# Repacking two transposed weights from six groups on 112 partitions to five groups on 128

## The chip, the cores and the metric

One core of one Trainium2 chip. The metric is the time of one execution on the device, in microseconds (us). Executions that the host times are some 2.1 us longer than the span that the profile shows (393.76 against 391.6 for the profiled run of before). In the clock records of the traces, TensorE's clock is granted either in full or in half; what sets it is called the clock gate here, and each run lists the share granted over the whole run. That share matters: runs with 0.996 to 1.0 are called undisturbed, and only those are compared where it is said so.

## The reference, cut to what matters

```python
def reference(A_x, A_wqkv, A_w_phi, A_wo, B_x, B_w1, B_w2, c, w_mod):
    # sa, ca, ga, sb, cb, gb = six rows of silu(c) @ w_mod
    h = _layernorm(x) * (1 + ca) + sa
    x = x + ga * attention(h)      # 32 heads of 18; pq = q @ w_phi[h], pk = k @ w_phi[h], softmax features
    h = _layernorm(x) * (1 + cb) + sb
    x = x + gb * ffn(h)            # relu, 576 -> 4608 -> 576
```

2048 tokens, 576 features, bf16. Since pq = (h @ wq) @ w_phi, the kernel folds w_phi into wq and wk once, head by head, ahead of the projections. ga is about 0.001 in size, so the attention branch hardly shows in the output.

## The kernel before: the parts concerned

The fold multiplies each group of transposed weight rows (as the stationary operand, 116 of its columns at a time, five such chunks) by a block-diagonal matrix of the heads' w_phi. Groups are cut so that none straddles head 16, where the output changes its PSUM bank.

```python
G6 = ((0, 6), (6, 6), (12, 4), (16, 6), (22, 6), (28, 4))     # first head, heads
GR = 108; GP = 112; R = 116; NC = 5; F = NC * R               # F = 580
wkT = carve(R1, 5800, (6, F))          # R1: one region, used by turns
wqT = carve(R1, 9280, (6, F))
...
load(sp, ccol[:], "cc"); load(sp, flat(wsc), "wsc")
load(sp, flat(wkT[0:GP]), "wkT")       # 112 rows of 6960 B
load_xT(0); load(sp, flat(wsh), "wsh"); load_x(0, 2) ...
...
def fold_all(wT):                      # keys: job FK, 30 matmuls
    for ck in range(NC):
        for g, (h0, nh) in enumerate(G6):
            pe.matmul(o, lhsT=wT[0:nf, g, ck * R:(ck + 1) * R], rhs=bdw[0:nf, g, 0:nf], ...)
def fold_mm(wT, ck, pr): ...           # queries: jobs FQ0..FQ4, one chunk each, 6 matmuls

w1a = carve(R1, 0, (4, DFF))           # DFF = 4608; quarter i is columns 4608*i to 4608*(i+1) of R1
def t_part(i, k):                      # VectorE: T1 = B12 - B11 and so on, 6 of 18 groups each
    eng.tensor_tensor(out=o[:, j, :], in0=p[:, j, :], in1=q[:, j, :], op=ALU.subtract)
# "wo" jobs, GpSimd: wo_sb[:, c, :] *= ga_row, five of them
```

The order of all jobs up to the feed-forward part is one written list. Of it, three stretches matter (Z: filler matmuls, which multiply zeros and whose results are not used, sc: modulation, FK: key fold, wl1: load of the second quarter of w1, tp: VectorE's subtractions, nO: attention output):

```python
Z11 sx sd rp sc FK ca Z2 fs0 fsr frr fra2 sh ...
... FQ2:0 pM5 K8:2 ... sp10 wl1 V7:0 ... FQ0:0 pA9 FQ4:2 ...
... tp0 wo4 qt1 kz Q4:1 eQ3 wo2 sq2 tp2 Q5:2 eQ4 sq3 tp1 wo3 nu0:3 eQ5 Q6:0 sq4 nO0 wo0 ...
```

The softmax here doesn't subtract the row's maximum and nothing guards it: scores larger than these inputs give would overflow.

Of the kernel before, what the change touches and what calls it, by code (L numbers as in the profile page):

```python
# [7 lines left out]
P = 128  # L8
BF16 = mybir.dt.bfloat16
# [7 lines left out]
S, D, H, DH, DFF = 2048, 576, 32, 18, 4608  # L17
NT = S // P
NC = 5
R = 116  # L20
F = NC * R
X0 = 96
NX = X0 + 4
NJ = DFF // P
HD = 288
NK = NJ // 2
G6 = ((0, 6), (6, 6), (12, 4), (16, 6), (22, 6), (28, 4))
GR = 108
GP = 112
BLK = ((0, 2), (2, 2), (4, 4), (8, 4), (12, 4))  # L30
E36 = 2 * DH
KVC = [((P * c) // E36, (P * c + P - 1) // E36) for c in range(9)]
# [30 lines left out]
def tile_block(ctx, tc, a, out):  # L63
# [7 lines left out]
    def small(shape, dtype, name):  # L71
        return mem.tile(shape, dtype, name=name, tag=name)

    def carve(reg, start, shape):
        n = 1
        for d in shape:
            n *= d
        names = "abcd"[:len(shape)]
        v = reg[:, start:start + n]
        return v.rearrange(f"p ({' '.join(names)}) -> p {' '.join(names)}", **dict(zip(names, shape)))  # L80

    x_sb = small([P, NT, D], BF16, "x_sb")
    R1 = small([P, 4 * DFF + DFF // 2], BF16, "R1")
# [17 lines left out]

    wsc = carve(R1, 0, (NC, F))
    wsh = carve(R1, 2900, (NC, F))
    wkT = carve(R1, 5800, (6, F))
    wqT = carve(R1, 9280, (6, F))
    wv_raw = carve(R1, 12760, (NC, D))
    wfold = carve(R1, 15640, (NC, D))
    wga = carve(R2[0], 0, (NC, D))
# [7 lines left out]
    mk = small([P, 1], FP32, "mk")  # L116
    mask = small([P, KVW], BF16, "mask")
    epsr = small([1, KVW + P], BF16, "epsr")
    RS = small([P, 6 * GR + NC * NX + NC * P], BF16, "RS")
    bdw = carve(RS, 0, (6, GR))  # L120
    m98 = carve(RS, 6 * GR, (NC, NX))
    rep = carve(RS, 6 * GR + NC * NX, (NC, 32))
    kvz = small([P, KVW], BF16, "kvz")
    ga_row = small([P, D], BF16, "ga_row")
    gb_row = small([P, D], BF16, "gb_row")
# [31 lines left out]
    PS = psum.tile([P, 8, 512], FP32, name="PS")  # L157
# [6 lines left out]
    act, dve, pool, sp, pe = nc.scalar, nc.vector, nc.gpsimd, nc.sync, nc.tensor  # L164
# [24 lines left out]
    def load_xT(b):  # L189
        t0, nt = BLK[b]  # L190
        xT, o, _, _ = XOFF[t0]
        i = t0 * NC * P
        sp.dma_start(xT[:, o:o + NC * nt * P], a["xT"][:, i:i + NC * nt * P])

    def load(eng, dst, name):
        eng.dma_start(dst, a[name])

    def flat(v):
        return v.rearrange("p a b -> p (a b)")

    load(act, flat(bdw[0:GP]), "bdw")
    load(act, ident[:], "ident")
    load(sp, ccol[:], "cc")
    load(sp, flat(wsc), "wsc")
    load(sp, flat(wkT[0:GP]), "wkT")
    load_xT(0)
    load(sp, flat(wsh), "wsh")
    load_x(0, 2)
# [2 lines left out]
    load_xT(1)  # L211
    load_x(4, 2)
    load(sp, epsr[:], "epsr")
    load(sp, flat(wqT[0:GP]), "wqT")
    load_xT(2)
    load(sp, flat(wcb), "wcb")
    load(sp, flat(wsb), "wsb")
# [35 lines left out]
                              rhs=siluc[0:R, ck:ck + 1], start=(ck == 0), stop=(ck == NC - 1))  # L253

    def fold_mm(wT, ck, pr):
        for g, (h0, nh) in enumerate(G6):
            k, c0 = divmod(h0 * DH, HD)
            nf = nh * DH
            pe.matmul(pr[0:R, k, c0:c0 + nf], lhsT=wT[0:nf, g, ck * R:(ck + 1) * R], rhs=bdw[0:nf, g, 0:nf],
                      start=True, stop=True)  # L260

    def v2(ap):
        return ap.rearrange("p (b f) -> p b f", b=2)
# [166 lines left out]
    G5, FW = 504, 72  # L430

    def fold_all(wT):

        for ck in range(NC):
            for g, (h0, nh) in enumerate(G6):
                nf, c0 = nh * DH, h0 * DH
                o = PS[0:R, ck, c0:c0 + nf] if g < 5 else PS[0:R, 5, FW * ck:FW * (ck + 1)]
                pe.matmul(o, lhsT=wT[0:nf, g, ck * R:(ck + 1) * R], rhs=bdw[0:nf, g, 0:nf], start=True, stop=True,  # L438
                          skip_group_check=True)

# [24 lines left out]
    A12, A22 = A2[:, :, 0, :], A2[:, :, 1, :]  # L465
    SS = RS[:, 0:6 * HD].bitcast(FP32).rearrange("p (a f) -> p a f", f=HD)
    X, Y, Z = 6, 4, 7
# [128 lines left out]
    def k_minus(t):  # L596
# [4 lines left out]

    ENG = {"d": dve, "a": act, "p": pool}
    fold_chunk = lambda c, pr: fold_mm(wqT, c, pr)
    ROWS = {"K": wfold, "V": wv_raw, "Q": wfold}
    ROWD = {"K": wk, "V": wv, "Q": wq}
# [7 lines left out]
        "sh": lambda: mods([wsh], None, R, 7, idle=6),  # L613
        "shc": lambda: dve.tensor_copy(m98[0:R, :, X0 + 3], PS[0:R, 7, 0:NC]),
        "FK": lambda: fold_all(wkT),
        "fs": lambda c: f_scaled(wk, c), "fsd": lambda c: f_scaled_d(wk, c),
        "frd": lambda c: f_raw(dve, c), "fra": lambda c: f_raw(act, c),
# [208 lines left out]
def _rows():  # L826

    r = list(range(464 + X0)) + [-1] * (NX - X0) + list(range(464 + X0, D))
    return r + [-1] * (F - len(r))

def _layout(inputs):
    import numpy as np
    g = {k: np.ascontiguousarray(np.asarray(v)) for k, v in inputs.items()}
    dt = g["A_x"].dtype
    rows = np.array(_rows())
    on = rows >= 0

    def pad(m, n):
        return np.concatenate([m, np.zeros((n - m.shape[0],) + m.shape[1:], dt)], axis=0)

    def feat(m):

        z = np.zeros((F, m.shape[1]), dt)
        z[on] = m[rows[on]]
        return pad(z.reshape(NC, R, -1).transpose(1, 0, 2), P)

    def cols(m):
        z = np.zeros((m.shape[0], F), dt)
        z[:, on] = m[:, rows[on]]
        return z  # L850

    def flat(m):
        return np.ascontiguousarray(m).reshape(m.shape[0], -1)

    x = g["A_x"].reshape(S, D)
    o = {"xk": flat(x.reshape(NT, P, D).transpose(1, 0, 2))}
    xt = feat(np.ascontiguousarray(x.T))
    o["xT"] = np.concatenate([flat(xt[:, :, t0 * P:(t0 + nt) * P]) for t0, nt in BLK], axis=1)
    o["cc"] = flat(feat(g["c"].reshape(D, 1)))
    wm = g["w_mod"]  # L860
    sec = [wm[:, i * D:(i + 1) * D] for i in range(6)]
    o["wsc"] = flat(feat(cols(sec[1])))
    o["wsh"] = flat(feat(cols(sec[0])))

    def dup(m):
        return np.concatenate([m, m[:, 512:]], axis=1)
    o["wsb"], o["wcb"] = flat(feat(dup(sec[3]))), flat(feat(dup(sec[4])))
    o["wga"], o["wgb"] = flat(feat(sec[2])), flat(feat(sec[5]))
    w = g["A_wqkv"]

    def groups(m):
        z = np.zeros((6, GR, m.shape[1]), dt)
        for i, (h0, nh) in enumerate(G6):
            z[i, :nh * DH] = m[h0 * DH:(h0 + nh) * DH]
        return flat(pad(z.transpose(1, 0, 2), GP))
    o["wqT"] = groups(np.ascontiguousarray(cols(w[:, 0:D].T.copy())))
    o["wkT"] = groups(np.ascontiguousarray(cols(w[:, D:2 * D].T.copy())))
    o["wv"] = flat(feat(w[:, 2 * D:]))
    bd = np.zeros((6, GR, GR), dt)
    for i, (h0, nh) in enumerate(G6):  # L880
        for h in range(nh):
            bd[i, h * DH:(h + 1) * DH, h * DH:(h + 1) * DH] = g["A_w_phi"][h0 + h]
    o["bdw"] = flat(pad(bd.transpose(1, 0, 2), GP))
    idm = np.zeros((P, P + 1), np.float32)
    idm[:, :P] = np.eye(P)
    idm[[X0 + 1, 29, 61, 93, 125], P] = -1.0
    o["ident"] = idm.astype(dt)
    mk = np.zeros((P, KVW), np.float32)
    ep = np.zeros((1, KVW + P), np.float32)
    ep[0, KVW:] = 1.0  # L890
    for c in range(9):
        k, p0 = KVO[c]
        p0 += KVN[0] * k
        for h in range(KVC[c][0], KVC[c][1] + 1):
            b = p0 + (h - KVC[c][0]) * VW
            r = np.arange(P)
            mk[(P * c + r) // E36 == h, b:b + VW] = 1.0
            ep[0, b + DH] = 0.5e-6
    o["mask"], o["epsr"] = mk.astype(dt), ep.astype(dt)
    wo = np.zeros((NC * P, D), dt)  # L900
    wo[:D] = g["A_wo"]
    o["wo"] = flat(wo.reshape(NC, P, D).transpose(1, 0, 2))
    w1 = g["B_w1"]
    o["w1a"] = flat(w1[:512].reshape(4, P, DFF).transpose(1, 0, 2))
    o["w1b"] = np.concatenate([w1[512:, :DFF // 2], w1[512:, DFF // 2:]], axis=0)
    w2 = g["B_w2"].reshape(NJ, P, D).transpose(1, 0, 2)
    o["w2a"], o["w2b"] = flat(w2[:, :18]), flat(w2[:, 18:])
    return {k: np.ascontiguousarray(v) for k, v in o.items()}
# [19 lines left out]
```

## Time and profile before

| | before |
|---|---|
| time, median of 3 runs | 393.49 us (393.40 to 393.77) |
| span of the profiled run | 391.6 us |
| key fold on TensorE | 9.016 to 10.603 us (first to last start), 30 matmuls |
| first use of the fold by VectorE | 10.84 us |
| TensorE reaches the feed-forward part | 94.38 us |
| packets of wkT, of wqT (mean time of one) | 377 ns, 407 ns |
| packets of wsh, 128 rows of 5800 B | 224 ns |

Packet times are those that the trace records for each row of a transfer. The columns of timelines are: start, duration, instruction, idle time before it and its cause. Two lines of TensorE's list of waits matter below. The columns of TensorE's list of waits are: who waited, for what, us in total, times, longest.

```profile
PE PS L529 <- DVE o_sb L399: 0.8, 1, 0.8
...
PE PS L438 <- DMA R<-in_wkT_dram: 0.5, 1, 0.5
```

The first is a wait for attention's output at 80 us. What stands behind it is this stretch of the timelines of VectorE and of GpSimd (start, duration, instruction, idle time before it and its cause):

```profile
74.93 4.07 DVE L474 TENSOR_TENSOR RT<-R 128x1728 f16<-128x1728 bf16 x2
...
79.30 0.76 DVE L399 TENSOR_TENSOR o_sb<-PS,rden 128x576 bf16<-128x576 f32 x1
...
74.76 7.83 POOL L637 TENSOR_TENSOR wo_sb<-wo_sb,ga_row 128x576 bf16<-128x576 bf16 x5 [1.59 <-DMA ga_row<-gatd]
```

Two subtractions take 2.02 and 2.13 us, while the same instruction took 1.13 at 72.95 us. They run beside the scaling of wo on GpSimd, which began 0.17 us before the first of the two.

### The profile page before, as it was taken

The page shows a single profiled execution, that of the slowest core. Times are in us where ns is not written, and L with a number is a line of the kernel's source. Part 1 is how long each engine was busy: PE and PEld are TensorE (multiplying, and loading weights), DVE is VectorE, ACT ScalarE, POOL GpSimd, SP SyncE. Part 2 cuts the span into 40 slices and gives each one's busy share as a digit, 9 for nine tenths or more (in the row PEclk, how much of TensorE's full clock was granted, in tenths as well). Part 3 has the DMA queues.
Part 4 walks back from the last instruction along what each step waited for, and adds up shares of the span by engine and source line. Part 5 has one row for each costly group of instructions (what it writes and reads, how often), then busy time and mean ns, then how long its engine had stood idle before and what let it go on. Part 6 is the DMA issues. An engine that isn't in the chain of part 4 may idle for free.

```text
span 391.6 us, 8916 instructions
## 1 busy us (share of the span) xinstructions
PE 383.3 (98%) x3697; PEld 311.2 (79%) x3698; DVE 244.9 (63%) x452; ACT 157.9 (40%) x360; POOL 142.4 (36%) x199
## 2 busy tenths in 40 slices
PE   7999999999999999999999999999999999999996
PEld 4777888878887887788878878887888788878874
DVE  0889998854779756573765567458555754653221
ACT  1797779689531133124213510431153123312510
POOL 2155858741101510741164035305510641072045
PEclk9999999999999999999999999999999999999999
DMA  7999929695621151124303311440141144010001
GB/s 259 355 413 415 424 64 357 180 309 179 169 64 35 38 119 31 35 60 109 35 20 90 80 35 32 107 65 19 47 93 35 23 63 58 18 33 33 3 0 32
DMA packets 49467, 44.41 MB, mean 113 GB/s; under 512 B 39361, under 2 KB 42034, under 8 KB 48658
## 3 DMA queue, kind: packets, MB, share of 16 engines
q1 hardware_dynamic: 49154, 43.66, 39.0%
q8 instruction: 29, 0.48, 0.5%
q10 hardware_dynamic: 272, 0.18, 0.2%
q14 instruction: 12, 0.10, 0.1%
HBM read 28.03 MB, written 6.49 MB: 88 GB/s over the span
## 4 chain that ended last, share of the span: by engine, by line
PE 89%; DVE 4%; POOL 2%; DMA 2%; ACT 1%; issue 1%; SPq 0%; POOLq 0%; DVEq 0%; ACTq 0%
PE PS L683 33%; PE PS L742 29%; PE PS L274 12%; PE PS L410 5%; PE PS L690 5%; DMA R<-in_wkT_dram 2%; PE PS L324 1%; PE PS L391 1%; POOL RH L754 1%; DVE RT L474 1%; DVE st L241 1%; ACT RT L279 1%; POOL x_sb L729 1%; PE PS L438 0%; POOL yt L728 0%
## 5 line engine op out<-in xcount | busy, mean ns | idle before, releaser
L683 PE MATMUL PS<-h,R 128*128 128x256 bf16 x1152 | 133.5, 273 | 0.0
L683 PEld LDWEIGHTS <-R 128*128 128x128 bf16 x1152 | 109.8, 98 | 17.6 <-issue 5.1
L742 PEld LDWEIGHTS <-RH 128*128 128x128 f16 x864 | 84.5, 98 | 21.8
L728 POOL TENSOR_TENSOR yt<-yt,gb_row 128x288 f32<-128x288 f32 x23 | 16.8, 729 | 167.4 <-DVE yt L727 167.4
L742 PE MATMUL PS<-R,RH 128*128 128x288 bf16 (+1 forms) x576 | 75.6, 286 | 0.0
L697 ACT ACTIVATE RH<-PS 128x256 f16<-128x256 f32 x72 | 27.6, 383 | 114.1 <-PE PS L690 107.4
L699 DVE SCALAR_TENSOR_TENSOR RH<-PS,RH 128x256 f16<-128x256 f32 x72 | 30.1, 418 | 68.0 <-ACT RH L697 68.0
L279 ACT ACTIVATE RT<-PS,rs 128x576 bf16<-128x576 f32 x64 | 42.9, 749 | 8.3 <-PE PS L274 7.3
L698 ACT ACTIVATE RH<-PS 128x512 f16<-128x512 f32 x72 | 42.9, 595 | 7.8 <-PE PS L683 6.5
L746 ACT ACTIVATE RS<-PS 128x288 f32<-128x288 f32 x24 | 9.8, 410 | 76.0 <-PE PS L742 76.0
L742 PE MATMUL PS<-RT,RH 128*128 128x288 f16 x288 | 37.9, 286 | 0.0
L274 PE MATMUL PS<-RH,R 116*128 116x288 bf16 x240 | 31.8, 286 | 0.5 <-ACT RH L631 0.5
L754 POOL TENSOR_TENSOR RH<-RH,RT 128x2304 f16<-128x2304 f16 x7 | 31.8, 4545 | 0.0
L274 PE MATMUL PS<-RH,RT 116*128 116x288 bf16 x240 | 31.7, 286 | 0.0
L274 PEld LDWEIGHTS <-R 116*128 116x128 bf16 x240 | 22.9, 98 | 6.4 <-issue 0.7
L274 PEld LDWEIGHTS <-RT 116*128 116x128 bf16 x240 | 22.7, 98 | 5.5
L420 DVE TENSOR_SCALAR xn<-x_sb,mv,rs 128x576 bf16<-128x576 bf16 (+1 forms) x28 | 22.4, 841 | 7.3 <-ACT rs L415 7.3
L729 POOL TENSOR_TENSOR x_sb<-yt,x_sb 128x288 bf16<-128x288 f32 x31 | 22.7, 732 | 5.9 <-DVE yt L725 4.1
L241 DVE BATCH_NORM_STATS2 st<-x_sb 128x6 f32<-128x288 bf16 x60 | 24.2, 445 | 0.5
L410 PE MATMUL PS<-wo_sb,oT 128*128 128x288 bf16 x160 | 22.5, 286 | 0.0
L284 DVE TENSOR_REDUCE Rk<-RT 128x64 f32<-128x1152 bf16 x16 | 21.2, 1332 | 1.4 <-ACT RT L279 1.4
L284 DVE TENSOR_REDUCE Rq<-RT 128x64 f32<-128x1152 bf16 x16 | 21.5, 1343 | 0.0
(115 smaller groups left out, 413.3 us busy)
## 6 DMA issues: line engine op xcount, KB each, us to landing
R<-in_w1a_dram SPq DMA_DIRECT2D x4, 1152.0 KB
eqd<-RT SPq DMA_DIRECT2D x14, 288.0 KB, 4.7
RT<-eqd SPq DMA_DIRECT2D x14, 288.0 KB, 2.8
R<-in_w2a_dram SPq DMA_DIRECT2D x3, 864.0 KB, 11.7
R<-in_w2b_dram SPq DMA_DIRECT2D x2, 1296.0 KB, 11.8
out_dram<-x_sb SPq DMA_DIRECT2D x15, 144.0 KB, 2.4
RT<-in_xT_dram SPq DMA_DIRECT2D x2, 640.0 KB
x_sb<-in_xk_dram SPq DMA_DIRECT2D x3, 288.0 KB
```

Of the source, the lines that this page charges most:

```text
L241: dve.bn_stats(out=s[:, hf, :], in_=x_sb[:, t, hf * HD:(hf + 1) * HD])
L274: pe.matmul(pr[:, k, 0:HD], lhsT=xt(t, ck), rhs=w[0:R, ck, k * HD:(k + 1) * HD], start=(ck == 0), stop=(ck == NC - 1))
L279: act.activation(out=E.rearrange("p (b h s e) -> p b h s e", b=2, s=2, e=DH)[:, :, :, s, :], in_=pr[:, :, 0:HD].rearrange("p b (h e) -> p ...
L284: dve.tensor_reduce(out=Rr, in_=E.rearrange("p (c e) -> p c e", e=DH), axis=AXX, op=ALU.add)
L410: pe.matmul(pr[:, k, 0:HD], lhsT=oT[:, t % 2, ci, :], rhs=wo_sb[:, ci, k * HD:(k + 1) * HD], start=(ci == 0 and not add_x), stop=(ci == NC ...
L683: pe.matmul(PS[:, 2 * u + hf, n * 256:n * 256 + 256], lhsT=w1a[:, ci, jj * P:(jj + 1) * P], rhs=hb[:, ci, :], start=(n == 0 and ci == 0), ...
L697: act.activation(out=A11[:, j, :], in_=lo[:, :, 0, :], func=ACT.Relu)
L698: act.activation(out=A2[:, j, :, :], in_=PS[:, 2 * u + 1, :].rearrange("p (n s f) -> p n s f", n=2, s=2), func=ACT.Relu)
L699: dve.scalar_tensor_tensor(out=U3[:, j, :], in0=lo[:, :, 1, :], scalar=0.0, in1=A11[:, j, :], op0=ALU.max, op1=ALU.subtract)
L729: pool.tensor_tensor(out=x_sb[:, t, c], in0=y, in1=x_sb[:, t, c], op=ALU.add)
L742: pe.matmul(PS[:, bank, 0:HD], lhsT=am[:, j, :], rhs=bm[:, j, :], start=first and j == 0, stop=(j % 9 == 8), skip_group_check=True)
L754: pool.tensor_tensor(out=A12, in0=A12, in1=U2, op=ALU.subtract)
```

## The change

Its intent is to load the two transposed weights as full 128-partition transfers, with seven heads to a group (126 rows) so that five groups are enough.

```diff
-G6 = ((0, 6), (6, 6), (12, 4), (16, 6), (22, 6), (28, 4))
-GR = 108
-GP = 112
+G7 = ((0, 7), (7, 7), (14, 7), (21, 7), (28, 4))
+GR = 126
-    wkT = carve(R1, 5800, (6, F))
-    wqT = carve(R1, 9280, (6, F))
+    wkT = carve(R1, 5800, (NC, F))
+    wqT = carve(R1, 8700, (NC, F))
-    load(sp, flat(wkT[0:GP]), "wkT")          # wqT, bdw alike
+    load(sp, flat(wkT), "wkT")                # 128 rows of 5800 B
     def fold_mm(wT, ck, pr):
-        for g, (h0, nh) in enumerate(G6): ... one matmul
+        for g, (h0, nh) in enumerate(G7):     # group 14..20 cut in two at head 16
+            cut = sorted({h0, min(max(16, h0), h0 + nh), h0 + nh})
+            for p, q in zip(cut, cut[1:]): ... one matmul
     def fold_all(wT):
-        for g, (h0, nh) in enumerate(G6):
+        for g, (h0, nh) in enumerate(G7):
```

More of the change, by code (lines that the diff above doesn't have):

```diff
@@ L118, in tile_block @@
     epsr = small([1, KVW + P], BF16, "epsr")
-    RS = small([P, 6 * GR + NC * NX + NC * P], BF16, "RS")
-    bdw = carve(RS, 0, (6, GR))
-    m98 = carve(RS, 6 * GR, (NC, NX))
-    rep = carve(RS, 6 * GR + NC * NX, (NC, 32))
+    RS = small([P, 6 * HD], BF16, "RS")
+    bdw = carve(RS, 0, (NC, GR))
+    m98 = carve(RS, NC * GR, (NC, NX))
+    rep = carve(RS, NC * GR + NC * NX, (NC, 32))
     kvz = small([P, KVW], BF16, "kvz")
@@ L199, in flat @@
         return v.rearrange("p a b -> p (a b)")
-    load(act, flat(bdw[0:GP]), "bdw")
+    load(act, flat(bdw), "bdw")
     load(act, ident[:], "ident")
@@ L213, in tile_block @@
     load(sp, epsr[:], "epsr")
-    load(sp, flat(wqT[0:GP]), "wqT")
+    load(sp, flat(wqT), "wqT")
     load_xT(2)
@@ L255, in fold_mm @@
     def fold_mm(wT, ck, pr):
-        for g, (h0, nh) in enumerate(G6):
-            k, c0 = divmod(h0 * DH, HD)
-            nf = nh * DH
-            pe.matmul(pr[0:R, k, c0:c0 + nf], lhsT=wT[0:nf, g, ck * R:(ck + 1) * R], rhs=bdw[0:nf, g, 0:nf],
-                      start=True, stop=True)
+        for g, (h0, nh) in enumerate(G7):
+            cut = sorted({h0, min(max(16, h0), h0 + nh), h0 + nh})
+            for p, q in zip(cut, cut[1:]):
+                k, c0 = divmod(p * DH, HD)
+                pe.matmul(pr[0:R, k, c0:c0 + (q - p) * DH], lhsT=wT[0:nh * DH, g, ck * R:(ck + 1) * R],
+                          rhs=bdw[0:nh * DH, g, (p - h0) * DH:(q - h0) * DH], start=True, stop=True)
     def v2(ap):
@@ L434, in fold_all @@
         for ck in range(NC):
-            for g, (h0, nh) in enumerate(G6):
+            for g, (h0, nh) in enumerate(G7):
                 nf, c0 = nh * DH, h0 * DH
-                o = PS[0:R, ck, c0:c0 + nf] if g < 5 else PS[0:R, 5, FW * ck:FW * (ck + 1)]
+                o = PS[0:R, ck, c0:c0 + nf] if g < 4 else PS[0:R, 5, FW * ck:FW * (ck + 1)]
                 pe.matmul(o, lhsT=wT[0:nf, g, ck * R:(ck + 1) * R], rhs=bdw[0:nf, g, 0:nf], start=True, stop=True,
@@ L871, in groups @@
     def groups(m):
-        z = np.zeros((6, GR, m.shape[1]), dt)
-        for i, (h0, nh) in enumerate(G6):
+        z = np.zeros((NC, P, m.shape[1]), dt)
+        for i, (h0, nh) in enumerate(G7):
             z[i, :nh * DH] = m[h0 * DH:(h0 + nh) * DH]
-        return flat(pad(z.transpose(1, 0, 2), GP))
+        return flat(z.transpose(1, 0, 2))
     o["wqT"] = groups(np.ascontiguousarray(cols(w[:, 0:D].T.copy())))
@@ L878, in _layout @@
     o["wv"] = flat(feat(w[:, 2 * D:]))
-    bd = np.zeros((6, GR, GR), dt)
-    for i, (h0, nh) in enumerate(G6):
+    bd = np.zeros((NC, GR, GR), dt)
+    for i, (h0, nh) in enumerate(G7):
         for h in range(nh):
             bd[i, h * DH:(h + 1) * DH, h * DH:(h + 1) * DH] = g["A_w_phi"][h0 + h]
-    o["bdw"] = flat(pad(bd.transpose(1, 0, 2), GP))
+    o["bdw"] = flat(pad(bd.transpose(1, 0, 2), P))
     idm = np.zeros((P, P + 1), np.float32)
```

## The prediction

> **What bounds the kernel now.** I read the page's busy row and slices first, then the chain that ended last in order of time, then the waits of TensorE, then timelines of the start and of the stretch in which the second packed weight (wqT, queries) is used.
>
> ```profile
> PE 383.3 (98%) x3697; PEld 311.2 (79%) x3698; DVE 244.9 (63%) x452; ACT 157.9 (40%) x360; POOL 142.4 (36%) x199
> ...
> PE 89%; DVE 4%; POOL 2%; DMA 2%; ACT 1%; issue 1%; SPq 0%; POOLq 0%; DVEq 0%; ACTq 0%
> ```
>
> TensorE is busy for 98% of the span and 89% of the chain is TensorE, nearly all in the feed-forward part and the projections, which the diff doesn't touch. What it does touch is at the head of the chain:
>
> ```profile
> 1.64 7.34 DMA R<-in_wkT_dram
> 8.97 0.04 issue
> 9.02 1.80 PE PS L438 x30
> 10.82 0.02 issue
> 10.84 0.53 DVE RH L618
> ```
>
> Columns are start, duration, what. The chain begins with the load of wkT, goes through the 30 small matmuls of the key fold (L438), then through VectorE (L618 and what follows it in VectorE's order: statistics, scaling, row corrections), then ScalarE, and reaches the dense projections at 23.73 us. Everything later hangs on that, so a start that comes earlier should move the end by as much. The wait of TensorE for wkT is shorter than the 7.34 us suggest:
>
> ```profile
> 8.18 0.38 PE L252 MATMUL PS<-siluc,R 116*116 116x1 bf16 x5
> ...
> 9.02 1.79 PE L438 MATMUL PS<-RS,R 108*116 108x108 bf16 x30 [0.46 <-DMA R<-in_wkT_dram]
> ```
>
> The 25 modulation matmuls (L252) stand ahead of the fold on the same engine. The last of them starts at 8.366 us in the trace (its modelled end is 8.56), and they follow each other every 53 ns. So the fold could start at about 8.42 with its data there, against 9.016: 0.60 us is the most that a faster wkT can give.
>
> **What the Trainium skill says.** (1) "DMA: Bandwidth & Descriptors", section "Why a DMA increments its semaphore by 16 and not by 1": the engine count is the largest number up to 16 that divides the slowest dimension, so 112 rows and 128 rows both use 16 engines, with 7 and 8 rows each. (2) The same page, "The descriptor swizzle": for 128 partitions each engine writes one SBUF port; "SBUF — State Buffer", section "Door 1: The DMA port swizzle", says which partitions share a port (32 apart). By its table, 112 rows load the even ports with 8 rows each and several odd ports with 4. No page gives a rate for 112 partitions. The trace does: wsc and wsh (128 rows of 5800 B) have packets of 260 and 224 ns on average, wkT and wqT (112 rows of 6960 B) 377 and 407 ns, though rows of 6912 B in 128 partitions (w2a) take 264 to 267 ns. So row length isn't what makes them slow; the row count is what is left. (3) "TensorE: Matmul & The Clock Gate", section "LDWEIGHTS (loading the stationary operand)": the load time goes with the columns, not the contraction rows. The trace agrees on the second half: loads of 108 x 116 and of 72 x 116 at L259 take 128 to 133 ns, all alike. The columns stay 116.
>
> **The change, part by part.**
>
> *wkT load.* Per engine 7 packets x 377 ns = 2.64 us now; 8 x 222 ns (the median of wsc and of wsh packets) = 1.78 us after: 0.86 us less. Its semaphore is complete at 8.97 now; after, about 8.1, below the 8.42 at which TensorE becomes free. So 0.60 us of the 0.86 counts on TensorE, and the DMA wait disappears.
>
> *Key fold.* 25 matmuls for 30. In the trace, first start 9.016, last start 10.603: 29 gaps of 54.7 ns, and within it groups of 108 columns and of 72 columns keep the same 160 ns per three. This is the pace of the weight loads (53 ns apart also where the moving operand has one column), not of the columns. 126 columns at the pace of the dense projections (288 columns every 122.5 ns) are 53.6 ns, so still about 54 ns each. Saved: 5 x 54.7 = 0.27 us, all on the chain.
>
> *bdw load* on ScalarE's queue grows from 112 x 1296 B to 128 x 1260 B, 16 KB more; its packets take 62 ns now and it is done by 3.2 us. Nothing.
>
> *Query fold* (L259). Group 3 (heads 14 to 20) straddles the PSUM bank border at head 16 and is cut in two, so it stays at 6 matmuls per chunk, 30 in all, and the same 576 columns. Nothing.
>
> *wqT load.* 7 x 407 ns = 2.85 us becomes 1.78: 1.07 us less. The query fold starts at 21.46 and wqT is complete at about 20.5, so it isn't waited for now; after, it comes near 18.6. With wkT's gain, all loads queued behind it come some 1.9 us earlier while the queue is full (to about 41 us). No TensorE wait there is on them. Nothing directly.
>
> *A moved address, which the title doesn't tell.* wqT now begins at column 8700 of the shared region, and the second quarter of the feed-forward weight covers columns 4608 to 9216. Before (9280) they did not meet. The built order shows it: this load (third of the w1a/w2a loads on the queue) now also waits for TensorE, namely for the query fold of chunk 2, and the folds of chunks 0 and 4 wait for the load to land. They then read 516 columns of group 0 that hold other weights: all of chunk 0's and part of chunk 4's for heads 0 to 6. That is a wrong value, in a branch which the reference multiplies by a gate of about 0.001, so the result should still pass. For time I checked both new waits:
>
> ```profile
> 30.85 0.33 SPq L558 DMA_DIRECT2D R<-in_w1a_dram  x1
> 39.39 0.33 SPq L550 DMA_DIRECT2D R<-in_w2a_dram  x1
> ...
> 41.23 0.48 PE L259 MATMUL PS<-RS,R 108*116 108x108 bf16 x6
> ...
> 49.76 0.80 PE L259 MATMUL PS<-RS,R 108*116 108x108 bf16 x12
> ```
>
> The load is issued at 30.85 now and lands at 44.3 to 46.4, behind a full queue. After, it is issued when the fold at 41.23 is over, near 41.0 with the earlier start; the queue is by then nearly empty (the load ahead of it lands at 43.6 now, 41.7 after). From issue to first data 1.3 us (wsc: issued 1.18, first packet 2.40), then 8 packets x 354 ns = 2.83 us, then a tail of up to 1 us among engines: 45.2 to 46.2. The folds that need it are due at 49.76 - 0.87 = 48.9. Slack about 2.7 us, so no stall. The two loads behind it land at about their old time (51.5 for the last), and the next queue user comes at 53.68.
>
> *Sum.* 0.60 + 0.27 = 0.87 us. What else gates the start: VectorE's statistics at 12.32 (11.45 after) need x, complete at 11.98 now, about 11.1 after; wv, complete at 13.76, comes near 12.9 for a use at 13.37; the shift modulation waits for wsh, 11.24 now and 10.4 after, 0.2 us later than TensorE wants it, but its result is first used at 14.22 (13.35 after), 0.5 us after it is ready. So the chain through VectorE can move by the whole 0.87 us. 393.49 - 0.87 = 392.62.
>
> **Rivals.** *The gain is swallowed*: another load becomes the last to arrive before VectorE needs it (x has only 0.3 us of margin), or ScalarE's 0.6 us evacuations set the pace. For: the margins are tenths. Against: VectorE runs without gaps from 10.84 to 17, so it is the only chain there. Time 393.0 to 393.4. *The new wait on the feed-forward load stalls TensorE*: for it, two waits that weren't there and a load that can't start until 41; against it, the 2.7 us of slack. If it landed 3 us later than I think it would cost under 1 us: 393. *More than the start is gained*, because all loads come 1.9 us earlier: against it, TensorE waits for no load but wsc and wkT anywhere in its list of waits, so 392.3 at best. *The transfer gain is less*, because the slow packets come from something other than the row count: then only the fold's 0.27 us is left, 393.2.
>
> **Range and chances.** The three runs before lie within 0.4 us. My central case is 392.6; partial loss reaches 393.3, full gain with luck in the later waits 392.0. 2% would be 7.9 us; nothing touched is that large, except a stall that I misjudged by three times its slack.
>
> **What would show it right or wrong.** In the changed profile: packets of wkT and wqT near 222 ns instead of 377 and 407; the fold at L438's successor starting at 8.4 with no DMA wait, 25 matmuls ending near 9.8; VectorE's first use at 9.95 to 10.0; the dense projection that starts at 23.73 starting near 22.9; the query folds of chunks 0 and 4 starting near 48.9 without a DMA wait; and every later landmark earlier by the same 0.9 us. Wrong would be: a DMA wait at the folds of chunks 0 and 4, a start that is earlier and a feed-forward part that isn't, or packets as slow as before.

## The result and the profile after

392.16 us median of 4 runs (391.92 to 392.93), against 393.56 of 4 runs before. The ratio is 0.9967 (95% interval 0.9950 to 0.9985); ratios here are the mean time of one kernel's fast runs over that of the other's of the same rounds, so not quite the ratio of the medians. That is 1.3 us less in the means (1.4 in the medians), where 0.87 was predicted, inside the range.

The head of the chain after, in the same columns as in the prediction:

```profile
8.81 0.22 PE PS L251 x5
9.03 1.46 PE PS L438 x25
10.49 0.02 issue
10.52 0.53 DVE RH L618
```

The transfer is gone from the head; TensorE's own modulation (L251) stands in its place. All waits of TensorE that are listed:

```profile
PE PS L235 <- POOL eps_t L227: 1.3, 1, 1.3
PE PS L268 <- DVE RS L614: 0.7, 1, 0.7
PE PS L274 <- ACT RH L631: 0.5, 1, 0.5
PE PS L577 <- DVE RH L481: 0.3, 1, 0.3
PE PS L410 <- POOL wo_sb L637: 0.2, 1, 0.2
```

No wait for wkT, none at the query folds, none for o_sb, and a new small one for wo_sb. The stretch behind the last two:

```profile
74.66 3.09 DVE L474 TENSOR_TENSOR RT<-R 128x1728 f16<-128x1728 bf16 x2
...
78.05 0.76 DVE L399 TENSOR_TENSOR o_sb<-PS,rden 128x576 bf16<-128x576 f32 x1
...
75.18 7.39 POOL L637 TENSOR_TENSOR wo_sb<-wo_sb,ga_row 128x576 bf16<-128x576 bf16 x5 [2.29 <-DMA ga_row<-gatd]
...
82.63 0.65 PE L410 MATMUL PS<-wo_sb,oT 128*128 128x288 bf16 x4 [0.19 <-POOL wo_sb L637]
```

VectorE's first subtraction of this stretch now starts 0.5 us before the scaling of wo and takes 1.04 us; only the second takes 2.13.

How much earlier each landmark is than in the profile of before, in us, for the profiles that the text uses. The first column is when the clock gate first gave TensorE its full clock in that execution, as the clock records of the trace say. "Fold" is from first to last start.

| profile | clock full at | fold starts | fold | VectorE's first use | TensorE at o transposed | feed-forward starts | last matmul |
|---|---|---|---|---|---|---|---|
| before | 5.09 | (9.02) | 1.59 | (10.84) | (80.12) | (94.38) | (387.41) |
| after | 7.30 | -0.12 | 1.39 | -0.33 | -1.20 | -0.86 | -0.91 |
| after_again | 6.43 | -0.53 | 1.39 | -0.74 | -1.27 | -1.27 | -1.32 |
| no_overlap | 4.09 | -0.71 | 1.39 | -0.92 | -1.33 | -1.33 | -1.38 |
| best | 6.67 | -0.42 | 1.39 | -0.63 | -1.50 | -1.51 | -1.56 |
| pad_only | 6.48 | -0.51 | 1.57 | -0.53 | -1.45 | -1.12 | -0.73 |
| before_tplate | 6.50 | -0.17 | 1.59 | -0.17 | -1.08 | -1.09 | -1.14 |
| pack_only | 7.13, half again 10.54 to 13.95 | +1.15 | 2.20 | +1.83 | +1.05 | +1.39 | +1.34 |
| before_again | 6.00, half again 9.41 to 23.07 | +0.99 | 2.94 | +2.41 | +5.14 | +5.48 | +5.43 |

The profiled run of the changed kernel was the slowest of its four (392.93): the clock came 2.2 us later than in the profile of before, so the modulation ahead of the fold ended 0.47 us later, and of the start only 0.33 us was left. Another 0.87 us came at o, and 0.34 went back into the wait for wo_sb (listed with 0.2 only, because the matmul before it counts as busy for part of that time). That pad_only gains 0.39 us less at its last matmul than at the start of the feed-forward part was not followed up.

### The profile page after: what moved, and what is told of

It reads as the page before. It is cut to its first block, busy times and chain, and to the rows that moved or that the text cites. A ratio compares the mean times of both kernels' runs of the same rounds, so it can differ in the third digit from the quotient of the medians.

```text
span 390.7 us, 8908 instructions
## 1 busy us (share of the span) xinstructions
PE 383.8 (98%) x3693; PEld 311.7 (80%) x3693; DVE 244.3 (63%) x452; ACT 157.9 (40%) x360; POOL 142.3 (36%) x199
## 4 chain that ended last, share of the span: by engine, by line
PE 86%; POOL 6%; ACT 2%; DVE 2%; DMA 2%; issue 1%; SPq 0%; POOLq 0%; DVEq 0%; ACTq 0%
PE PS L683 33%; PE PS L742 29%; PE PS L274 9%; PE PS L410 5%; PE PS L690 5%; POOL wo_sb L637 2%; PE PS L235 2%; PE PS L391 1%; ACT RT L279 1%; POOL RH L754 1%; DMA gatd<-gt 1%; PE PS L324 1%; POOL RT L291 1%; DMA ga_row<-gatd 1%; DVE st L240 1%
```

## The experiments

Each ran with the kernel before on the same chip. Three sets of rounds: the runs with a granted clock of 0.996 or more of the kernel before have means of 393.59, 393.32 and 393.77 us (6, 7 and 7 runs of 11 each). The other 13 of these 33 runs had 0.981 to 0.995 and 394.4 to 399.7 us, and one of them 0.755 and 496 us. The first set of before (4 runs, no clocks on record) had none over 393.77. Because the printed ratios mix both kinds (6 of these 13 runs count as fast), the text compares undisturbed runs. A run at 0.996 may still have lost one window of clock: the profile of pack_only, below, is such a run. Before has one at 0.996 in the first of these sets (394.89 us) and one in the third (394.84 us). Without them its means are 393.32, 393.32 and 393.59 us, so the gains of after_again, no_overlap and pad_only, which are 1.21, 1.32 and 1.08 us against 393.59, become 0.95, 1.05 and 0.82 us.

**after_again** is the changed kernel, unedited.

> The changed kernel, unedited, once more. Theory (three parts): the start gives 0.3 us when TensorE's clock rises late, as in the profile taken (spins at 427 ns until 6.4 us), and 0.8 to 0.9 us when it rises near 5.1 us as in the profile of before; VectorE's subtraction at 74.66 gets ahead of GpSimd's scaling of wo (0.87 us more, duration 1.04 us in place of 2.02); 0.2 to 0.35 us is given back in a TensorE wait for the scaled wo. Expected time 391.9 to 392.3, ratio 0.9960 to 0.9970. If a clock that rises late were all that limits the start, a profile with an early rise should show the fold's end 0.85 us earlier than before. Rival: the VectorE part is chance of one profile; then this run's profile shows GpSimd first and 2.0 us again, and the time is nearer 392.7.

Measured: 391.74 to 393.03, mean 392.38 of six, all undisturbed, 1.21 us under the kernel before of its rounds (printed ratio 0.9936, with low-clock runs of before in it). In the profile the start is 0.74 us earlier, and GpSimd came first this time, by 0.73 us (73.49 against 74.23): the first subtraction waited only for the rest of the running 1.27 us and took 1.45. So "VectorE first" is not a property of the changed kernel. The second part of the theory, that its 0.87 us is simply a gain, fell; what holds is that the stretch varies between executions. The third part fell too: there is no wait for wo_sb in this profile.

**no_overlap** puts wqT back where nothing shares its columns.

```diff
-    wqT = carve(R1, 8700, (NC, F))
+    wqT = carve(R1, 9280, (NC, F))
```

> wqT back at column 9280, so that it no longer shares columns with the feed-forward load; five groups and 128 rows kept. Theory (the moved waits cost and gain nothing): same time as the changed kernel within 0.2 us, feed-forward load issued near 28 to 31 us again, no DMA wait of TensorE. Rival (the late feed-forward load is what moved the scaling of wo later and let VectorE go first): the row for wo lands about 0.7 us earlier relative to VectorE, the subtraction takes 2.0 us again, and the time is 392.6 to 392.8.

Measured: 391.84 to 392.91, mean 392.27 of six undisturbed runs, 0.1 us from after_again. The feed-forward load goes out at 28.45 us again, against 41.19 in the changed kernel:

```profile
28.45 0.33 SPq L558 DMA_DIRECT2D R<-in_w1a_dram  x1
```

```profile
41.19 0.33 SPq L558 DMA_DIRECT2D R<-in_w1a_dram  x1
```

The first line is no_overlap's queue, the second the changed kernel's. The time doesn't differ, and in neither does TensorE wait for a load at the query folds, so the two new waits are free, as predicted. The rival's second half, GpSimd early and first, did come (73.43 against 74.04), but in after_again with the overlap too, and without the loss. In no_overlap the clock was full at 4.09 us, and the start is 0.92 us earlier: the predicted 0.87 within 0.05, with the two terms at 0.71 and 0.20.

**pad_only** keeps six groups and pads to 128 rows.

```diff
-GP = 112
+GP = 128
```

> The kernel before, six groups of at most 108 rows, but wkT, wqT and bdw padded to 128 partitions in DRAM and loaded so: 14% more bytes. Theory (the row count makes the packets slow): packets of 6960 B at 265 to 275 ns in place of 377 and 407, so 8 x 267 = 2.14 us per engine in place of 2.64; wkT there near 8.5, fold at 8.4 to 8.6 if the clock rises early, still 30 matmuls of 54.7 ns; start gain 0.4 to 0.6 us. Rival (the row length of 6960 B is what is slow): packets stay at 370 to 410 ns, wkT comes later than before (8 packets instead of 7), and the time is 393.5 to 394.

Measured: packets of 6960 B at 272 and 269 ns, no wait for wkT, fold still 1.57 us, start 0.53 us earlier; mean 392.50 of six undisturbed runs, 1.08 us under the kernel before. TensorE's timeline has the 30 matmuls, without a wait before them:

```profile
8.50 1.77 PE L438 MATMUL PS<-RS,R 108*116 108x108 bf16 x30
```

So it is the 112 rows that were slow, not the 6960 B, and 14% more bytes in 128 rows arrive sooner. Most of the change's gain comes without any repacking. The small rows of bdw show no such effect: 112 rows of 1296 B took 62 ns each before, and 128 of them 61 ns here.

**pack_only** packs as the change does and loads in 112 and 16 rows.

```diff
-    load(sp, flat(wkT), "wkT")                       # wqT alike
+    sp.dma_start(flat(wkT[0:112]), a["wkT"][0:112])
+    sp.dma_start(flat(wkT[112:P]), a["wkT"][112:P])
```

> The changed kernel's packing in five groups and its addresses, but wkT and wqT each loaded by two transfers, of 112 and of 16 rows. Theory (112 rows make packets slow whatever their length): the 112-row part has packets of 5800 B at 310 to 345 ns instead of 222; wkT is there at 8.7 to 9.0; the fold starts then and has 25 matmuls; start gain 0.3 to 0.5 us (0.27 of it from the fold's five matmuls). Rival (6960 B, not 112 rows, was slow): the packets take 222 ns and the start is as in the changed kernel.

Measured: the packets took 373 ns (wkT) and 386 ns (wqT) with 5800 B, as slow as with 6960 B. The expected 310 to 345 ns scaled with length and was wrong: in 112 rows a packet takes about the same at both lengths. The packets of the two 16-row transfers took just as long, 384 and 383 ns, also those that started when the 112 rows were done; so 112 is not a special number, and what they have in common is that neither fills 128 rows. Why that makes packets slow isn't shown. Repacking with such transfers gains nothing: 393.21 us in the one run with a clock of 0.999, 394.93 to 399.37 in the other five. This is not quite repacking alone, as the fold now waits for two transfers, and the 16 rows land last. Its profile (394.93 us, 0.996) shows more of why it is slow:

```profile
7.24 0.43 PE L253 MATMUL PS<-siluc,R 116*116 116x1 bf16 x5 [0.65 <-DMA R<-in_wsc_dram]
...
10.17 2.46 PE L440 MATMUL PS<-RS,R 126*116 126x126 bf16 x25 [0.67 <-DMA R<-in_wkT_dram]
```

(TensorE's timeline; line numbers are shifted by 2.) wsc, which stands ahead in the queue and was not changed, is also reported complete late (at 7.20 us, though its last packet ended at 5.46), and the fold of 25 takes 2.46 us instead of 1.58, because the clock was halved from 10.54 to 13.95.

**before_delay** puts a small GpSimd copy ahead of the scaling, in the kernel before.

```diff
-tp0 wo4 qt1
+tp0 pd wo4 qt1
+        "pd": lambda: pool.tensor_copy(pd_t[:], ga_row[:, 0:160]),
```

> The kernel before, with one small GpSimd copy (128 x 160 of the gate row) put ahead of its scaling of wo, which moves that start by some 0.3 us behind VectorE's subtraction. Theory (whichever of the two starts first holds the other up, and this decides 0.7 to 0.9 us in either kernel): the first subtraction after kvz takes 1.04 us in place of 2.02, VectorE comes to o 0.8 to 0.9 us earlier, TensorE's 0.76 us wait for o_sb goes, some of it returns as a wait for wo; time 392.8 to 393.1. Rival (the 2.02 us is not a matter of who starts first): the subtraction stays at 2.0 us and the time is 393.5 or more.

Measured: in the profile VectorE was first by 0.06 us, and both subtractions ran unhindered:

```profile
74.71 2.13 DVE L475 TENSOR_TENSOR RT<-R 128x1728 f16<-128x1728 bf16 x2
```

```profile
74.77 1.16 POOL L650 COPY pd_t<-ga_row 128x160 bf16<-128x160 bf16 x1 [1.82 <-DMA ga_row<-gatd]
75.90 7.01 POOL L638 TENSOR_TENSOR wo_sb<-wo_sb,ga_row 128x576 bf16<-128x576 bf16 x5
```

2.13 us for two, against 4.07: who starts first decides. The first subtraction takes 1.04 us where it starts first; where a scaling operation is already running and has 0.54, 0.67 or 1.11 us left (after_again, no_overlap, before), it takes 1.45, 1.58 or 2.02, that is 0.91 us and the rest of that operation. Here the small copy stood between, and itself took 1.16 us. TensorE's wait for o_sb is gone, 0.45 us of it returns as a wait for wo_sb. The time doesn't confirm a gain: the four undisturbed runs are 393.47 to 394.85, mean 394.21, 0.6 us above the kernel before. That the order sets the subtraction's time is shown, the expected time of the kernel is missed; why the other three undisturbed runs are 0.5 to 1.4 us slower than the profiled one isn't known, as they left no trace.

**before_tplate** moves two of the subtractions to where VectorE is idle.

```diff
-... sq2 tp2 Q5:2 eQ4 sq3 tp1 wo3 nu0:3 ... nO1 oc0 ... ap1 Q13:2
+... sq2 Q5:2 eQ4 sq3 wo3 nu0:3 ... nO1 tp2 oc0 ... ap1 tp1 Q13:2
```

> The kernel before; the second and third of VectorE's three subtractions (6 of 18 groups each) are taken out of the stretch in which GpSimd scales wo and put where VectorE is idle: behind the second o, and behind the second normalisation (idle 81.4 to 84.2 and 90.6 to 92.2 us in the profile of before). Theory (these two against the scaling of wo hold TensorE up by 0.76 us in the kernel before): o_sb 2 to 3 us earlier, the 0.76 us wait of TensorE for o_sb gone, the scaling five times 1.27 us without a long one, the start unchanged; fast runs near 392.7, so 0.6 to 0.8 us under the kernel before. Rival (that wait is covered by another one close behind): the wait moves to wo_sb or to the attention's next step, 393.2 to 393.5.

Measured: the profile does what was expected: subtractions of 1.08 and 1.05 us, wo scaled in 6.20 us instead of 7.83, no wait for o_sb, and 0.91 us gained between the start (-0.17) and o (-1.08). But five undisturbed runs have a mean of 393.15, only 0.17 us under the kernel before. So the 0.76 us wait in the one profile of before is probably not what an average execution pays. In the profiles of before_spin and before_again, which have the same code there, it is absent.

**best** is no_overlap with the same move.

> The changed kernel with wqT at 9280 and the same move of the two subtractions. Theory (the start and the subtractions are two gains that add up when the second is no longer left to who comes first): 0.8 to 0.9 plus 0.76, so 391.7 to 392.0 in fast runs, and a narrower spread than the changed kernel's. Rival (the changed kernel has already all of it): within 0.1 us of the changed kernel, 392.2 to 392.4.

Measured: 391.53 to 392.40, mean 391.90 of six undisturbed runs, 1.42 us under the kernel before of its rounds; printed ratio 0.9938 (0.9890 to 0.9986). Its profile has both gains:

```profile
76.76 0.76 DVE L399 TENSOR_TENSOR o_sb<-PS,rden 128x576 bf16<-128x576 f32 x1
...
80.54 1.05 DVE L474 TENSOR_TENSOR RT<-R 128x1728 f16<-128x1728 bf16 x1
```

```profile
73.68 6.22 POOL L637 TENSOR_TENSOR wo_sb<-wo_sb,ga_row 128x576 bf16<-128x576 bf16 x5 [1.09 <-DMA ga_row<-gatd]
```

It beats the kernel before. Against the changed kernel it ran on different chips, 0.2 us apart when each is measured from its own before; whether that is real stays open.

**before_spin** fills TensorE's wait for wkT with filler matmuls.

```diff
-sx sd rp sc FK
+sx sd rp sc Z2 FK
```

> The kernel before, with two more filler matmuls (2 x 0.213 us) on TensorE between the modulation and the key fold, that is in the 0.46 us in which it waits for wkT. Theory (the slow runs of 397 to 399 us, granted clock 0.981 to 0.987, of the kernel before come from that wait: TensorE looks idle in one window of 3.41 us and is given half its clock for one or more windows): no run under 0.995 in six, where the kernel before has some 4 in 10; fast runs as before, 393.1 to 393.7. Rival (the slow runs have nothing to do with the start): 2 or 3 slow runs in six.

Measured: two of six runs at 0.981 and 0.983 (398.96 and 399.68 us). The cure failed. The slow runs left no trace. In the profile of an undisturbed one wsc came so late that TensorE waited 1.3 us for it, and still 0.5 us for wkT after the fillers, so the fillers did not fill the waits:

```profile
7.03 0.43 PE L252 MATMUL PS<-siluc,R 116*116 116x1 bf16 x5 [1.33 <-DMA R<-in_wsc_dram]
...
10.22 1.79 PE L438 MATMUL PS<-RS,R 108*116 108x108 bf16 x30 [0.48 <-DMA R<-in_wkT_dram]
```

The clock was full from 4.66 us on all the same. The four undisturbed runs have a mean of 394.00.

**before_again** is the kernel before, one profile. It caught a slow run.

> The kernel before, unedited, one more profile. Theory (TensorE's 0.76 us wait for o_sb depends on which of VectorE's subtraction and GpSimd's scaling of wo comes first by tenths of a microsecond, and differs between executions): the wait is anything from 0 to 0.8 us; the two subtractions together take 3.0 to 4.1 us; TensorE waits 0.2 to 0.6 us for wkT. Rival (it is a fixed property of the kernel before): 0.7 to 0.8 us and 4.0 to 4.1 us again.

Measured: 399.19 us, granted clock 0.983. The two subtractions took 3.09 us with VectorE first, and there was no wait for o_sb: the theory of a varying stretch holds, the rival falls. And this is what a slow run looks like (stretches: us from the start, then busy us and instructions of PE, PEld, DVE, ACT, POOL, then the granted clock, DMA share, GB/s):

```profile
6.00:9.00 3.00, 2.27 (x27) 1.55 (x26) 0.00 (x0) 0.00 (x0) 0.19 (x1) 1.00 0.95 233
9.00:12.00 3.00, 2.35 (x26) 2.26 (x25) 0.34 (x2) 0.69 (x2) 0.00 (x0) 0.57 1.02 389
12.00:15.00 3.00, 3.00 (x22) 2.19 (x21) 1.74 (x4) 3.00 (x6) 0.00 (x0) 0.50 1.01 408
```

```profile
10.01 3.21 PE L438 MATMUL PS<-RS,R 108*116 108x108 bf16 x30 [0.65 <-DMA R<-in_wkT_dram]
```

The second fence is TensorE's timeline. The clock gate gave full clock at 6.00, took half of it back at 9.41, one 3.41 us window later, and kept it for 13.65 us, four windows. In the window from 6.00 TensorE had waited 0.73 us for wsc and then run the thin modulation matmuls; of the 0.65 us wait for wkT only the first 0.05 us lies in it.

**after_gap** takes the five fillers among the modulation out of the changed kernel.

```diff
-        "sc": lambda: mods([wsc], None, R, 7, idle=6),
+        "sc": lambda: mods([wsc], None, R, 7),
```

> The changed kernel with the five filler matmuls among the modulation taken out, so that TensorE is there before wkT again and waits for it 0.3 to 0.7 us; the fold starts at 8.2 to 8.5 as in the changed kernel. Theory (a wait of TensorE there puts its clock at risk): some of the six runs have a granted clock of 0.98 to 0.996 and 394 to 399 us, though the DMA is as fast as in the changed kernel; the others 392.0 to 392.6. Rival (the slow runs come with the 112-row transfers or with the chip): none of the six is slow.

Measured: clocks of 0.994, 0.987 and 0.993 in three of six runs (392.82, 396.26 and 393.83 us); the others 391.81 to 392.81. In the profile TensorE waited 0.74 us for wsc and 0.36 us for wkT, and had half its clock from 7.35 to 10.76:

```profile
5.87 1.49 PE L251 MATMUL PS<-siluc,R 116*116 116x1 bf16 x25 [0.74 <-DMA R<-in_wsc_dram]
7.72 2.80 PE L438 MATMUL PS<-RS,R 126*116 126x126 bf16 x25 [0.36 <-DMA R<-in_wkT_dram]
```

These two loads have 128 rows here, so a low clock doesn't need the 112-row transfers, and the rival falls. What it does need can be read from the three profiles that caught one. TensorE's busy time in the 3.41 us before the clock was halved doesn't tell them apart: it was 2.62 (before_again), 2.67 (after_gap) and 2.62 us (pack_only), but 2.65 in no_overlap's and 2.09 in before_spin's first window at full clock, and both kept it. The columns do, if one adds up those of the moving operand over the matmuls that started in the window: 2073, 2073 and 2901, where no other window at full clock up to 25 us, in any of the 14 profiles, has fewer than 3085. The 25 thin matmuls of the modulation bring one column each, a filler 512. No experiment varied the columns alone, so this is a reading of the traces, not a shown cause.

**probe_overlap** and **probe_clean** fold the query weight's chunk 0 once more early and write 1000 times the difference of both foldings into 116 rows of the output.

```diff
-FQs1 kv1 ... FQs0 w2b0
+FQs1 px:2 pxs kv1 ... FQs0 pxd w2b0
+        "px": lambda: fold_chunk(0, at["px", None]),
+        "pxd": lambda: dve.tensor_tensor(out=px_t[0:R, :], in0=wq[0:R, 0, :], in1=px_t[0:R, :], op=ALU.subtract),
```

> Wrong output on purpose, at the changed kernel's addresses: the query weight's chunk 0 is folded once more early, before the feed-forward load that shares its columns is issued, and 1000 times the difference of the two foldings is written in place of 116 rows of the output. If the load overwrites the weight before its use, the difference is not zero: values of the order of 1 to 15, an error far above the largest input. If the order protects it, all 116 rows are zero and the largest error is that of x left out, 0.2 or so.

> Wrong output on purpose, as probe_overlap, with wqT at column 9280 where nothing shares its columns. If the overlap caused the difference of the two foldings, it is now zero in all 116 rows and the relative error is that of x left out in 116 of 2048 rows, about 0.24 (the root of 116/2048) if it is taken in the root mean square; if the difference has another cause, the error is near the 7.96 of probe_overlap again.

Measured: relative error 7.96 at the changed kernel's addresses, 0.239 with wqT at 9280, where the root of 116/2048 is 0.238. So the changed kernel does fold feed-forward weights into part of its queries (chunk 0 was tested). It passes against the reference all the same, as the factor ga, called the gate in the recorded texts, hides the branch. No time depends on it, but no one should take over the change with that address.

## Why the prediction was right or wrong

- *wkT's transfer*: right. 226 ns a packet for 222 expected, complete at 7.90 us for 8.1. pad_only and pack_only show that the number of rows does it, not their length.
- *What it overlooked there*: wsc, ahead in the queue and unchanged, is reported complete at 6.19 to 7.20 us in the six profiles with 112-row transfers behind it and at 5.83 to 6.17 in the eight with 128, though its last packet ends at 5.1 to 5.9 us in both. So the row count probably moves the modulation's start as well, which the sum took as fixed. No experiment separates this.
- *TensorE free at 8.42, 0.60 us of the start*: right for a clock like that of before (0.71 in no_overlap, where the modulation also began 0.11 earlier; 0.53 in after_again), 0.12 in the profile of the change. The sum took the moment at which TensorE's clock rises as given. It differed by 3.2 us between no_overlap (4.09) and the changed kernel (7.30), whose folds start at 8.30 and 8.89.
- *Key fold, 0.27 us*: mis-sized. The 25 matmuls, of 126 and 72 columns, stand 57.9 ns apart (1.39 us in 24 gaps), not 54, so it is 0.20 us. That the pace is "not of the columns" holds for the mean of three matmuls before, but within the three the gaps are 70, 53 and 37 ns, the short one behind 72 columns; in the changed kernel those behind 126 columns are mostly 57 to 59.
- *Query fold, bdw, the new waits*: right. The late feed-forward load went out at 41.19 for 41.0 and was complete at 46.41 for 45.2 to 46.2; the folds that need it came at 49.46 without a wait. (From issue to first data the prediction's own two figures give 1.22 us, not 1.3; nothing hangs on it.)
- *"every later landmark earlier by the same 0.9 us"*: wrong, and with it the dismissal of the rival that more than the start is gained. TensorE's wait for o_sb, 0.76 us, stood in the list that was read for DMA waits alone, and the sum let it move along. It hangs on a race between VectorE and GpSimd, whose starts differ by tenths between profiles, and it was absent from both profiles of the changed kernel and 0.3 us in no_overlap. Between the two profiles this was 0.87 us of the 0.91, with 0.34 given back.
- *The measured 1.3 us against the predicted 0.87*: the range held it. In the rounds of after_again it is 1.21, or 0.95 without the run at 0.996, so how much there is beyond 0.87 isn't settled. before_tplate gives the race 0.17 us on average. VectorE's first use of the fold in the four full-clock profiles with 112 rows lies at -0.21 (before_delay), -0.17, 0 and +1.20 us (before_spin) against that of before, and in the six with five groups and all fillers at -0.33 to -1.07. The means differ by 1.0 us, so the average gain of the start may be a little larger than 0.87. That is argued from few profiles, and that the number came out near the prediction is in part luck: in the profiled pair the start gave 0.33 us and the race most of the rest.
- *Not foreseen at all*: the low-clock runs. None among 24 runs of after_again, no_overlap, pad_only and best; 13 among the 33 of the kernel before in rounds beside these and the other experiments, 5 among 18 of before_delay, before_tplate and before_spin, 4 of 6 of pack_only. Part of what the change is worth on some chips is that it removes them. before_again shows the clock falling after a window with a wait for wsc and thin matmuls, after_gap that taking fillers out brings this back without slow transfers. That the wait for wkT is the trigger isn't shown: putting fillers there did not help.

## What to carry to other kernels

Try loading weights as 128 rows even if that means padding: it paid here with rows of 5800 and 6960 B, while rows of 1296 B took the same time each in 112 as in 128. Look at the time of one packet, not at bytes alone. In a list of waits, a wait on another engine at the far end of the kernel is part of the forecast too: ask whether it would move along or change. And before placing a tensor elsewhere in a region that is used by turns, look at who else writes there: the overwritten queries passed the comparison with the reference.

## What the Trainium skill lacked or had wrong

- "DMA: Bandwidth & Descriptors" ("Why a DMA increments its semaphore by 16 and not by 1") gives, by its rule, 16 engines for 112 rows as for 128, and no page says what 112 rows cost: 366 to 459 ns a packet for rows of 5800 or of 6960 B, against 222 to 227 and 269 to 272 in 128 rows. By these numbers 7 packets in a row take 2.6 to 3.2 us, where 8 take 1.8 or 2.2. The transfer ahead of them in the queue, wsc, was reported complete later too: at 6.19 to 7.20 us against 5.83 to 6.17.
- "TensorE: Matmul & The Clock Gate" ("What's actually happening") says that idle TensorE gets half its clock after an idle window of some 3.4 us. The windows of 3.41 us are seen here. But no wait that long was needed: in before_again a single wait of 0.73 us and the thin matmuls behind it were enough, with TensorE busy for 2.62 of the 3.41 us, and the low clock lasted 13.65 us.
- The same section lets the rise vary by 500 ns in either direction. It came between 3.94 (after_gap) and 7.30 us here, by the traces' clock records, a spread of 3.36 us.
- "SBUF — State Buffer" ("Who interferes with whom") says that two-input VectorE operations block against GpSimd reads, whoever comes second. That agrees: 1.04 us when VectorE was first, 2.02 when it was second. It doesn't say that a stream of GpSimd operations holds up each following VectorE operation once, and is itself held up: 2.08 us in place of 1.27.
